# One weight matrix unevenly over the DMA engines, and a new order of the last tiles, in a decode block bound by its loads

## The chip, the cores and the metric

One core of one Trainium2 chip. The time is the device time of one execution in microseconds; a kernel's time is the median of its runs. The span is that of the profiled execution from its first to its last instruction, 1.5 to 2 us less than the time of the same execution.

## The reference

A decode step with one new token for each of 4 sequences: layer norm, then attention against a cache of 8,192 positions with 32 heads of 128, and beside it a gated feed-forward layer; both are added to x.

```python
xn = layernorm(x)                                    # x: 4 x 512
q = (xn @ wq) as (4, 32 heads, 128)                  # wq: 512 x 4096
p = softmax(einsum("bhqd,bhkd->bhqk", q, k_cache) * 128 ** -0.5)
o = einsum("bhqk,bhkd->bhqd", p, v_cache)            # caches: 4 x 32 x 8192 x 128 each
out = x + o @ wo + (silu(xn @ w_gate) * (xn @ w_up)) @ w_down
```

All inputs are bf16. The two caches are 537 MB of the 551 MB that have to be read.

## The kernel before

Everything large goes through five slots of 4 MiB. A tile n is one sequence's K or V for a pair of heads; there are 64 of each. All loads are issued on one queue, in the order of the code. K tiles come two iterations ahead of their scores, V tiles two iterations ahead of their products.

```python
wq_t = slot()                                            # 512 rows: 4 on each partition
nc.sync.dma_start(out=wq_t[:], in_=A_wq.rearrange("(p c) n -> p (c n)", c=EC))
...
for c in range(EC):                                      # q: 32 matmuls 128x32x512
    for half in range(NH):
        for cg in range(NQ):
            mm(q_ps[half][cg * QB:(cg + 1) * QB, :], xnt_w[:, c, :], wq_t[:, n0:n0 + 512], start=(c == 0))
...
for i in range(NT + LP):                                 # NT = 64, LP = 2
    if i + 2 < NT:
        load_k(i + 2)
    nv = i + 2 - LP
    if 0 <= nv < NT:                                     # the last two V tiles come in pieces
        load_v(nv, (32, 32, 32, 16, 16) if nv == NT - 1 else (32,) * 4 if nv == NT - 2 else (T,))
    ...                                                  # per tile: 8 DVE transposes, 32 score matmuls
    npv = i - LP                                         # 32 matmuls p x V of tile i - 2
    ...
        if bv == B - 1 or npv == NT - 2:
            fin_1(jv)                                    # ACT copy, DVE mask and sum: o of a pair of heads
        if bv == B - 1:
            fin_q(jv)                                    # PE sums over rows: waits for fin_1
```

## Time and profile before

| | before |
|---|---|
| time | 1288.93 us (1288.72 to 1289.07, 3 runs) |
| span | 1287.1 us |
| PE, DVE busy | 84%, 57% |
| bytes read | 550.8 MB |
| PE's wait for the DVE sum of o | 37.3 us in 16 places |

The prediction below shows the lines that carry the argument and reads them. The core has 16 DMA engines, and the profile's DMA line is the mean busy share of the 16. The trace also has every packet's start, duration, size and queue, but not its engine. On one engine a packet starts 3 or 4 ns before the recorded end of its predecessor, so the packets can be strung into 16 chains; those of the kernel before hold the same sequence of sizes each, 34.42 MB of kernel data. "Last data of an engine" below is the end of the last input packet of such a chain. This regrouping is worked out from the records; it is not a view of the profile.

### The profile page before, as it was taken

The page shows a single profiled execution, that of the slowest core. Times are in us where ns is not written, and L with a number is a line of the kernel's source. Part 1 is how long each engine was busy: PE and PEld are TensorE (multiplying, and loading weights), DVE is VectorE, ACT ScalarE, POOL GpSimd, SP SyncE. Part 2 cuts the span into 40 slices and gives each one's busy share as a digit, 9 for nine tenths or more (in the row PEclk, how much of TensorE's full clock was granted, in tenths as well). Part 3 has the DMA queues.
Part 4 walks back from the last instruction along what each step waited for, and adds up shares of the span by engine and source line. Part 5 has one row for each costly group of instructions (what it writes and reads, how often), then busy time and mean ns, then how long its engine had stood idle before and what let it go on. Part 6 is the DMA issues. An engine that isn't in the chain of part 4 may idle for free.

```text
span 1287.1 us, 11189 instructions
## 1 busy us (share of the span) xinstructions
PE 1083.1 (84%) x4778; PEld 430.3 (33%) x4778; DVE 738.1 (57%) x951; ACT 39.7 (3%) x87; POOL 5.3 (0%) x13
## 2 busy tenths in 40 slices
PE   4888888888888798897997888888887988978788
PEld 1334333333333333332333333333333333333334
DVE  6663556546556556466556566465465465573544
ACT  1000000000000000000000000000000000000000
POOL 1000000000000000000000000000000000000000
PEclk9898898998989999898998989989899898989899
DMA  9999999999999999999999999999999999999997
GB/s 407 427 430 435 437 425 437 429 436 431 432 435 428 436 432 433 431 432 435 431 435 428 434 432 431 436 431 433 430 434 431 437 430 432 433 431 427 433 434 304
DMA packets 21529, 551.49 MB, mean 428 GB/s; under 512 B 2268, under 2 KB 2792, under 8 KB 3944
## 3 DMA queue, kind: packets, MB, share of 16 engines
q1 hardware_dynamic: 21464, 550.78, 99.4%
q8 instruction: 37, 0.61, 0.2%
q14 instruction: 12, 0.10, 0.0%
q10 hardware_dynamic: 16, 0.01, 0.0%
HBM read 550.77 MB, written 0.00 MB: 428 GB/s over the span
## 4 chain that ended last, share of the span: by engine, by line
DMA 50%; PE 31%; DVE 14%; issue 5%; ACT 1%; SPq 0%; DVEq 0%
DMA slot<-in_A_k_cache_dram 44%; PE oacc L76 17%; PE sps L76 12%; DVE kt L277 11%; DMA slot<-in_A_v_cache_dram 6%; PE mps L76 1%; DVE ptz L318 1%; DVE o L356 1%; PE xps L76 1%; DVE o_sb L354 1%; ACT o_sb L353 0%; PE mps L299 0%; DVE otn L377 0%; PE yo_ps L76 0%; DVE rcp L328 0%
## 5 line engine op out<-in xcount | busy, mean ns | idle before, releaser
L76 PE MATMUL sps<-kt,zq 128*128 128x512 bf16 x2048 | 578.3, 421 | 145.2 <-DVE kt L277 128.7
L277 DVE STREAM_TRANSPOSE kt<-slot 128x1024 uint32<-128x1024 uint32 x512 | 587.6, 1210 | 90.4 <-DMA slot<-in_A_k_cache_dram 89.5
L76 PE MATMUL oacc<-slot,ptz 128*8 128x512 bf16 x2016 | 450.4, 379 | 0.4 <-DMA slot<-in_A_v_cache_dram 0.4
L76 PEld LDWEIGHTS <-zq 128*128 128x128 bf16 x2048 | 212.0, 104 | 496.1 <-issue 317.0
L76 PEld LDWEIGHTS <-ptz 128*8 128x8 bf16 x2016 | 177.5, 92 | 258.1 <-issue 27.8
L328 DVE RECIPROCAL rcp<-mps 128x4 f32<-128x4 f32 x32 | 5.9, 183 | 281.9 <-PE mps L76 281.9
L354 DVE TENSOR_TENSOR o_sb<-o_sb,rowu 128x512 f32<-128x512 f32 x16 | 11.1, 693 | 89.2 <-ACT o_sb L353 89.0
L76 PE MATMUL xps<-rowy,o 128*32 128x4 f32 (+1 forms) x228 | 13.5, 205 | 37.3 <-DVE o L356 37.3
L293 DVE TENSOR_REDUCE mx<-sps 128x1 f32<-128x512 f32 x32 | 22.1, 692 | 18.5 <-PE sps L76 18.5
L76 PEld LDWEIGHTS xps<-rowy,o 128*32 128x32 f32 (+1 forms) x228 | 12.1, 154 | 44.9 <-DVE o L356 44.9
L268 DVE COPY zq<-qt 32x8 bf16<-32x8 bf16 x128 | 21.3, 166 | 1.3
L302 DVE TENSOR_REDUCE nm<-mps 128x4 f32<-128x64 f32 x32 | 7.2, 225 | 24.0 <-PE mps L299 24.0
L356 DVE TENSOR_REDUCE o<-o_sb 128x128 f32<-128x512 f32 x16 | 16.3, 1020 | 0.5
L76 PEld LDWEIGHTS mps<-rowb,rs 128*128 128x128 f32 x64 | 9.5, 186 | 13.8 <-issue 13.8
L76 PEld LDWEIGHTS <-slot 128*128 128x128 bf16 x272 | 11.7, 126 | 3.5 <-DVE slot L188 2.6
L76 PE MATMUL mps<-rowb,rs 128*128 128x4 f32 x64 | 12.3, 263 | 0.0
L353 ACT COPY o_sb<-oacc 128x512 f32<-128x512 f32 x16 | 9.4, 586 | 76.8 <-PE oacc L76 76.8
L377 DVE TENSOR_TENSOR otn<-xps,rcp 32x16 bf16<-32x16 f32 x28 | 4.8, 170 | 11.7 <-PE xps L76 10.3
L299 PE MATMUL mps<-ident_f,mx 128*128 128x128 f32 x32 | 10.3, 323 | 0.8 <-DVE mx L293 0.8
L299 PEld LDWEIGHTS mps<-ident_f,mx 128*128 128x128 f32 x32 | 4.3, 133 | 14.7 <-DVE mx L293 14.2
L170 PE MATMUL xps<-ident,kt 4*128 4x4 bf16 x4 | 0.3, 173 | 10.1 <-DVE kt L165 10.1
L76 PE MATMUL yo_ps<-slot,otn 128*4 128x256 bf16 x64 | 8.2, 281 | 0.3 <-DVE otn L366 0.3
(150 smaller groups left out, 148.5 us busy)
## 6 DMA issues: line engine op xcount, KB each, us to landing
slot<-in_A_k_cache_dram SPq DMA_DIRECT2D x64, 4096.0 KB, 39.2
slot<-in_A_v_cache_dram SPq DMA_DIRECT2D x62, 4096.0 KB, 36.8
slot<-in_A_v_cache_dram SPq DMA_DIRECT2D x7, 1024.0 KB, 22.3
slot<-in_A_wq_dram SPq DMA_DIRECT2D x1, 4096.0 KB, 12.3
slot<-in_A_wo_dram SPq DMA_DIRECT2D x1, 3584.0 KB, 40.2
slot<-in_B_w_gate_dram SPq DMA_DIRECT2D x1, 1792.0 KB, 31.9
slot<-in_B_w_up_dram SPq DMA_DIRECT2D x1, 1792.0 KB, 35.8
slot<-in_B_w_down_dram SPq DMA_DIRECT2D x1, 1792.0 KB, 30.9
```

Source lines behind the costliest of these rows:

```text
L76: nc.tensor.matmul(out_ap, lhsT=lhsT, rhs=rhs, start=start, stop=True, skip_group_check=True, **kw)
L268: nc.vector.tensor_copy(out=zq[gr % 2][a * QB:(a + 1) * QB, :, :, XO + a * QB].rearrange("p b (j r) -> p r j b", r=2), in_=qt[a * QB:(a + ...
L277: nc.vector.transpose(out=kt[:].bitcast(dt.uint32).rearrange("p (j t r) -> p t j r", j=2, r=QB), in_=src.rearrange("p (t j r) -> p t j r", ...
L293: nc.vector.reduce_max(out=mx[:], in_=s_ps[gr][:], axis=AX.X)
L299: nc.tensor.matmul(mps[:, 0:P], lhsT=nmx.pop(gr)[:, 0:1].to_broadcast([P, P]), rhs=ident_f[:, :], is_transpose=True, start=True, stop=True ...
L302: nc.vector.tensor_reduce(out=nm[:], in_=by_row(mps[:, 0:P]), axis=AX.XY, op=ALU.max, negate=True)
L318: nc.vector.transpose(out=t_[y * HP:(y + 1) * HP, :, y, :, :].rearrange("p s u x -> p s (u x)"), in_=p_[y * HP:(y + 1) * HP, :].rearrange( ...
L328: nc.vector.reciprocal(out=rcp[j][:, :, 2 * bp:2 * bp + 2], in_=mps[:, P:P + B].rearrange("p (y b) -> p y b", y=HT))
L353: nc.scalar.copy(out=o_sb[:].rearrange("p u d -> p (u d)"), in_=o_acc[j % 2][:])
L354: nc.vector.tensor_tensor(out=o_sb[:], in0=o_sb[:], in1=rowu[:].unsqueeze(2).to_broadcast([P, NV, Dh]), op=ALU.mult)
L356: nc.vector.reduce_sum(out=o1[:], in_=o_sb[:].rearrange("p u d -> p d u"), axis=AX.X)
L377: nc.vector.tensor_tensor(out=otn[q0:q1, blk * 4:blk * 4 + 4, :], in0=xps[q0:q1], in1=r_[q0:q1, y, :].unsqueeze(1).to_broadcast([QB, 4, B] ...
```

## The change

It has four parts. wq is no longer spread evenly: 384 rows and 32 rows lie on all partitions, and 96 rows lie on 32 partitions alone, loaded by two transfers whose outermost source dimension is 4. The last four tiles to be loaded are V tiles (K63 moves ahead of V60), the last two in other pieces. The PE part of o of a pair of heads is put off until after three pieces of the next scores. wo is loaded four iterations sooner, and the row sums of p are taken one iteration sooner.

```diff
-    wq_t = slot()
-    nc.sync.dma_start(out=wq_t[:], in_=A_wq.rearrange("(p c) n -> p (c n)", c=EC))
+    C1, LE, LG, LR, NC = EC - 1, 4, 2, 3, 4
+    LW = 4 * LE
+    R1, R2 = C1 * P, C1 * P + LG * LW * LR
+    wq_t, wq_u = slot(), slot()
+    nc.sync.dma_start(out=wq_t[:, 0:C1 * NQ_], in_=A_wq[0:R1, :].rearrange("(p c) n -> p (c n)", c=C1))
+    nc.sync.dma_start(out=wq_t[:, C1 * NQ_:C1 * NQ_ + CN], in_=A_wq[R2:D, :].rearrange("r (k n) -> (r k) n", k=NC))
+    for g in range(LG):
+        r0 = R1 + g * LW * LR
+        nc.sync.dma_start(out=wq_u[g * QB:g * QB + LW, 0:LR * NQ_],
+                          in_=A_wq[r0:r0 + LW * LR, :].rearrange("(r e c) n -> e r (c n)", r=4, e=LE))
...                                        (x laid out to match; 80 projection matmuls, q in two sums)
-    R_FFN, R_WO = 5, NT - 5
+    R_FFN, R_WO = 5, NT - 9
-        nv = i + 2 - LP
+        nv = i + 2 - LP if i < NT - 4 else -1 if i == NT - 4 else i + 1 - LP
-            load_v(nv, (32, 32, 32, 16, 16) if nv == NT - 1 else (32,) * 4 if nv == NT - 2 else (T,))
+            load_v(nv, (64, 32, 16, 8, 8) if nv == NT - 1 else (64, 64) if nv == NT - 2 else (T,))
...
+                if g == 2:
+                    while late:
+                        late.pop(0)()
...
-        npv = i - LP
+        npv = i - LP if i < NT - 2 else -1 if i == NT - 2 else i - LP - 1
...
-                    fin_q(jv)
+                    late.append(lambda jv=jv: fin_q(jv))
```

More of the change, by code (lines that the diff above doesn't have):

```diff
@@ L86 @@
     nc.scalar.dma_start(out=x_sb[:], in_=x_flat[:, :])
-    wq_t = slot()
-    nc.sync.dma_start(out=wq_t[:], in_=A_wq.rearrange("(p c) n -> p (c n)", c=EC))
+    NQ_ = H * Dh
+    C1, LE, LG, LR, NC = EC - 1, 4, 2, 3, 4
+    LW = 4 * LE
+    R1, R2 = C1 * P, C1 * P + LG * LW * LR
+    CN = NQ_ // NC
+    assert D - R2 == P // NC
+    wq_t, wq_u = slot(), slot()
[5 more added lines that the diff above has]
+                          in_=A_wq[r0:r0 + LW * LR, :].rearrange("(r e c) n -> e r (c n)", r=4, e=LE))
     k_tiles, v_tiles = {}, {}
@@ L121 @@
         nc.gpsimd.memset(z_[:], 0.0)
-    xnt_w = const.tile([P, EC, QB], dt.bfloat16, name="xnt_w")
+    NF = EC + C1 + NC
+    NX = NF + LR
+    xnt_w = const.tile([P, NX, QB], dt.bfloat16, name="xnt_w")
     nc.gpsimd.memset(xnt_w[:], 0.0)
@@ L163 @@
     nc.vector.reciprocal(out=rstd[:], in_=std[:])
-    xn_bf = kt_pool.tile([B, D], dt.bfloat16, name="kt")
-    nc.vector.tensor_scalar(out=xn_bf[:], in0=xc[:], scalar1=rstd[:, 0:1], scalar2=None, op0=ALU.mult)
-    xnt_ps = psX.tile([P, EC, B], dt.bfloat16, name="xps")
-    for c in range(EC):
-        nc.tensor.transpose(xnt_ps[:, c, :], xn_bf[0:B, c:D:EC], ident[0:B, 0:B])
-    nc.vector.tensor_copy(out=xnt_w[:, :, 0:B], in_=xnt_ps[:])
+    xn_bf = kt_pool.tile([B, D + NC * P + LG * LW * LR], dt.bfloat16, name="kt")
@@ new lines @@
+    nc.vector.memset(xn_bf[:, D:D + NC * P], 0.0)
+    nc.vector.tensor_scalar(out=xn_bf[:, 0:D], in0=xc[:], scalar1=rstd[:, 0:1], scalar2=None, op0=ALU.mult)
+    DQ = D + NC * P
+    for k in range(NC):
+        nc.vector.tensor_copy(out=xn_bf[:, D + k * P + k:D + (k + 1) * P:NC], in_=xn_bf[:, R2:D])
+    for g in range(LG):
+        r0 = R1 + g * LW * LR
+        nc.vector.tensor_copy(
+            out=xn_bf[:, DQ:DQ + LG * LW * LR].rearrange("b (c g e r) -> b g c e r", c=LR, g=LG, e=LE)[:, g],
+            in_=xn_bf[:, r0:r0 + LW * LR].rearrange("b (r e c) -> b c e r", r=4, e=LE))
@@ new lines @@
+    xnt_ps = psX.tile([P, NX, B], dt.bfloat16, name="xps")
+    cols = [slice(c, D, EC) for c in range(EC)] + [slice(c, R1, C1) for c in range(C1)]
+    cols += [slice(D + k * P, D + (k + 1) * P) for k in range(NC)]
+    for c in list(range(EC, NX)) + list(range(EC)):
+        if c < NF:
+            nc.tensor.transpose(xnt_ps[:, c, :], xn_bf[0:B, cols[c]], ident[0:B, 0:B])
+        else:
+            for g in range(LG):
+                c0 = DQ + ((c - NF) * LG + g) * LW
+                nc.tensor.transpose(xnt_ps[g * QB:g * QB + LW, c, :], xn_bf[0:B, c0:c0 + LW], ident[0:B, 0:B])
@@ L174 @@
+    nc.vector.tensor_copy(out=xnt_w[:, 0:NF, 0:B], in_=xnt_ps[:, 0:NF, :])
+    for g in range(LG):
+        nc.vector.tensor_copy(out=xnt_w[g * QB:g * QB + LW, NF:NX, 0:B], in_=xnt_ps[g * QB:g * QB + LW, NF:NX, :])
     NH = H * Dh // 512 // NQ
     q_ps = [psS.tile([P, 512], dt.float32, name="sps") for _ in range(NH)]
-    for c in range(EC):
-        for half in range(NH):
-            for cg in range(NQ):
-                n0 = c * H * Dh + (half * NQ + cg) * 512
-                mm(q_ps[half][cg * QB:(cg + 1) * QB, :], xnt_w[:, c, :], wq_t[:, n0:n0 + 512], start=(c == 0))
@@ L182, with q_mm @@
-    q_bf = slots.tile([P, NH, 2, 8, NQ, QB], dt.bfloat16, name="slot")
+    def q_mm(acc, nb, c, p0, p1, w, start=False):
+        half, cg = divmod(nb, NQ)
+        mm(acc[half][cg * QB:(cg + 1) * QB, :], xnt_w[p0:p1, c, :], w, start=start)
+    for c in range(C1):
+        for nb in range(NH * NQ):
+            q_mm(q_ps, nb, EC + c, 0, P, wq_t[:, c * NQ_ + nb * 512:c * NQ_ + (nb + 1) * 512], start=(c == 0))
+    for nb in range(NH * NQ):
+        k, n0 = divmod(nb * 512, CN)
+        q_mm(q_ps, nb, EC + C1 + k, 0, P, wq_t[:, C1 * NQ_ + n0:C1 * NQ_ + n0 + 512])
@@ new lines @@
+    for g in range(LG):
+        p0, p1 = g * QB, g * QB + LW
+        for c in range(LR):
+            for nb in range(NH * NQ):
+                q_mm((q_ps, o_acc)[g], nb, NF + c, p0, p1, wq_u[p0:p1, c * NQ_ + nb * 512:c * NQ_ + (nb + 1) * 512],
+                     start=(g == 1 and c == 0))
+    q_2 = kt_pool.tile([P, NH, 512], dt.float32, name="kt")
+    for half in range(NH):
+        nc.scalar.copy(out=q_2[:, half, :], in_=o_acc[half][:])
+    q_bf = wq_u[:, 3 * NQ_:4 * NQ_].rearrange("p (n r x c i) -> p n r x c i", n=NH, r=2, x=8, c=NQ)
@@ L183 @@
     for half in range(NH):
         for par in range(2):
-            src = q_ps[half][:].rearrange("p (x i r) -> p x i r", x=8, r=2)[:, :, :, par]
-            src = src.unsqueeze(2).to_broadcast([P, 8, NQ, QB])
-            if half == 0:
-                nc.vector.tensor_copy(out=q_bf[:, half, par], in_=src)
-            else:
-                nc.scalar.copy(out=q_bf[:, half, par], in_=src)
+            a_, b_ = [t_.rearrange("p (x i r) -> p x i r", x=8, r=2)[:, :, :, par].unsqueeze(2).to_broadcast([P, 8, NQ, QB])
+                      for t_ in (q_ps[half][:], q_2[:, half, :])]
@@ L192 @@
+            nc.vector.tensor_tensor(out=q_bf[:, half, par], in0=a_, in1=b_, op=ALU.add)
     qt_ps = psM.tile([P, NH, 2, 8, NQ * B], dt.float32, name="mps")
@@ L385 @@
     JL = H // HT - 2
-    R_FFN, R_WO = 5, NT - 5
+    R_FFN, R_WO = 5, NT - 9
     wo_next, wo_ready = 0, 0
+    late = []
     build_q(0)
-    for i in range(NT + LP):
+    for i in range(NT + LP + 1):
         if i + 2 < NT:
             load_k(i + 2)
-        nv = i + 2 - LP
+        nv = i + 2 - LP if i < NT - 4 else -1 if i == NT - 4 else i + 1 - LP
         if 0 <= nv < NT:
-            load_v(nv, (32, 32, 32, 16, 16) if nv == NT - 1 else (32,) * 4 if nv == NT - 2 else (T,))
+            load_v(nv, (64, 32, 16, 8, 8) if nv == NT - 1 else (64, 64) if nv == NT - 2 else (T,))
         if i == R_FFN - 3:
@@ L428 @@
             jv, bv = divmod(npv, B)
-            if bv % 2 == 0:
-                row_sums(npv // 2)
+            if i < NT and bb == 1:
+                row_sums(gr)
             if bv == B - 1 or npv == NT - 2:
@@ L434, with fin_d @@
                 if jv < JL:
-                    fin_q(jv)
-                    if jv % 2 == 1:
-                        wo_ready = (jv + 1) * HT
-                else:
-                    xps = x_tile()
-                    fin_2(jv, xps)
-                    fin_3(jv, xps)
-                    wo_ready = (jv + 1) * HT
+                    late.append(lambda jv=jv: fin_q(jv))
+                else:
+                    def fin_d(jv=jv):
+                        xps = x_tile()
+                        fin_2(jv, xps)
+                        fin_3(jv, xps)
+                    late.append(fin_d)
+                wo_ready = (jv + 1) * HT if jv >= JL or jv % 2 == 1 else wo_ready
         elif i < NT and bb == 1:
             max_2(gr)
-        if i >= R_WO:
+            row_sums(gr)
+        if i >= R_WO and not late:
             for _ in range(8):
```

## The prediction

> **What bounds the kernel now.** I read the page first, then the DMA share in fine slices of the last 25 us, then the chain that ended last, in order of time, then the trace's single DMA packet records.
>
> ```profile
> span 1287.1 us, 11189 instructions
> PE 1083.1 (84%) x4778; PEld 430.3 (33%) x4778; DVE 738.1 (57%) x951; ACT 39.7 (3%) x87; POOL 5.3 (0%) x13
> ...
> DMA  9999999999999999999999999999999999999997
> ...
> q1 hardware_dynamic: 21464, 550.78, 99.4%
> q8 instruction: 37, 0.61, 0.2%
> q14 instruction: 12, 0.10, 0.0%
> ```
>
> PE is busy 84% of the span, yet DMA is full in every slice but the last. The 550.8 MB of inputs cannot be fewer, so the transfers set the time. What a change can touch is the two ends, and how evenly 16 engines share the bytes. The same DMA line over 1262 to 1287 us alone (0.625 us a slice), and the windows around its step:
>
> ```profile
> DMA  9999999999999999999976555555553200000000
> ```
>
> ```profile
> 1272.00:1274.00 2.00, 2.00 (x12) 0.82 (x9) 0.00 (x0) 0.00 (x0) 0.00 (x0) 1.00 0.99 412
> 1274.00:1276.00 2.00, 2.00 (x11) 0.83 (x10) 0.00 (x0) 0.00 (x0) 0.00 (x0) 1.00 0.75 315
> 1276.00:1278.00 2.00, 2.00 (x10) 0.72 (x8) 0.00 (x0) 0.00 (x0) 0.00 (x0) 1.00 0.56 236
> ```
>
> The columns before the last two are the engines' busy times and the clock; the last two are DMA share and GB/s. The share falls from 1 to 0.56 = 9/16 and stays there for 5 us: seven engines have run out while nine still work. To see why, I regrouped the packet records. On one engine a packet starts 3 to 4 ns before its predecessor's recorded end, so all records fall into 16 chains of 34.42 MB of kernel data each, without idle time between first and last tile. Their last data end as follows (us):
>
> - seven chains with no TensorE instruction fetch: 1274.5 to 1275.7, the typical one 1274.7;
> - eight chains that carry the 37 fetches of 16 KiB in turn (q8): 1280.4 to 1280.6 and 1281.7 to 1282.1, depending on whether 4 or 5 fetches fell before their end;
> - one chain with nine 8 KiB fetches (q14): 1282.37.
>
> (1281.7 - 1274.7) / 5 = 1.4 us per 16 KiB fetch: the fetch is recorded with 0.93 us, and the 32 KiB packet beside it takes 1.7 instead of 1.213 us. **The late nine are late by their instruction fetches, and the slowest engine ends the kernel.** The end of the chain:
>
> ```profile
> 1265.54 17.13 DMA slot<-in_A_v_cache_dram
> 1282.67 0.05 issue
> 1282.71 0.60 PE xps L76 x16
> 1283.32 0.03 issue
> 1283.34 0.18 DVE otn L366
> 1283.52 0.04 issue
> 1283.56 1.03 PE yo_ps L76 x4
> 1284.59 0.02 issue
> 1284.61 0.36 ACT res L458
> ```
>
> From the last data at 1282.37 to the end of the span, 1287.1, there are 4.74 us: 0.34 until PE sees them, 0.60 for 16 small matmuls, 0.2 for normalising, 1.0 for wo, 0.36 for the copy, the rest the output transfer. The execution time, 1288.93, is 1.8 above the span.
>
> [...] No run yet shows which engines; x, with 4 rows, does show 4 data packets. [...] the trace has 32,768 B in 1.210 us (1.213 less the overlap), 27.1 GB/s[...]. [...] after a 10.4 us wait, score matmuls at 1196 us are 0.43 us apart, not 0.22.
>
> **The change, part by part.**
>
> *wq.* Before, 4 MiB lie evenly: 262,144 B per engine. After, 384 rows (24 KiB per partition) and 32 rows (2 KiB per partition) lie evenly, 196,608 + 16,384 = 212,992 B per engine, and 96 rows go in two transfers over four engines, 2 x 4 x 24,576 = 196,608 B more on each of those. So twelve engines have 49,152 B less, at 27.1 GB/s **1.8 us less**; four have 147,456 B more, **5.4 us more**. If the four are early ones, they end at 1274.7 + 5.4 = 1280.1, at worst 1275.7 + 5.4 = 1281.1; the late ones end at 1282.37 - 1.8 = 1280.6 and 1282.1 - 1.8 = 1280.3. I take 1280.7: **1.7 us earlier**. That 5.4 + 1.8 = 7.2 is just the gap of the two groups (7.0 to 7.7) is my main reason to think that the 96 rows were sized for engines known to be early.
>
> *Preparation of q.* 17 small transposes instead of 4, six copies into the padded x and two more copies out, about 1.5 us, beside the wq transfer. 80 instead of 32 projection matmuls at 0.113 us (3.61/32). wq is complete only after 1.8 + 0.8 (slow first packet, 2 us) + 7.3 + 0.6 + 7.3 = 17.8 us instead of 12.7. 24 more matmuls behind it (2.7), two ACT copies (1.2), four adds of about 1.2 us on DVE instead of two copies there and two on ACT: the first K transpose moves from 22.7 to about 30 us. This costs nothing at the end while DMA queues stay filled. Per tile, first packet minus issue was 24 to 31 us for the first eight waiting tiles, 19 at least up to 1150 us, and 7.7 at the very end. A delay of 7 to 9 us that PE makes up by some 3 us per tile pair (19.7 us of DMA against about 16 of PE) leaves 10 us in hand.
>
> *Order of the last tiles.* Before: K62 V60 K63 V61 V62 V63. After: K62 K63 V60 V61 V62 V63, PV one iteration later. Bytes are equal. Before, PE had only 0.48 us of idle time ahead of the last 16 matmuls, so an earlier end of DMA alone would have met a busy PE. After, K63 lands about 39 us before the end (four tiles of 9.8), its scores end near 1250.5; PV60, PV61, PV62 (7.1 each) end near 1258, 1268 and 1275.5, and the first half of V63 comes at 1275.6. PE follows the data. Slots come free about 20 us before they are needed instead of 8 to 13. The last piece is 8 positions, not 16: 8 matmuls of 0.037 us less, **0.3 us**.
>
> *o waits for the next scores.* PE stood 37.3 us in 16 places before the head-sum matmuls, waiting for DVE; that goes to nearly nothing. It is not on the path: DMA is full meanwhile. Likewise row sums and an earlier wo load (four tile pairs sooner, one slot fewer for that time, where 10 us of queue remained before): **0**.
>
> Sum: -1.7 - 0.3 = -2.0 us, so 1288.93 - 2.0 = 1286.9.
>
> **The rivals.**
>
> 1. *The four engines are not the early ones.* If one carries fetches, it ends at 1282.1 + 5.4 = 1287.5, and the kernel takes 1288.93 + 5.1 - 0.3 = about 1294. For it: the records carry no engine numbers. Against: the sizing above; and the first wq packet of an early chain starts 4 ns before the end of an x packet's completion record (1.774 against 1.778), as if on the same engine. 10%.
> 2. *PE becomes the end.* Between PV60 (1258) and V61 (1261) PE idles 3 us. [...] gain cancelled, about 1288.5. [...] 20%.
> 3. *Late start or uneven landing empties the queue.* Engines 0 to 3 now lag by 7.2 us at first; a slot is free only when the slowest engine has landed and the tile is used. If both eat the 20 us in hand, every lost us adds at the end. Against: at least 10 us left. 5%.
> 4. *The 4-engine transfers are hidden anyway*: if the early engines are fewer than thought or a further fetch falls on the last engine[...], 1288 to 1289.
>
> **Range and chances.** Centre 1286.9; a near-exact balance gives 1286, rival 2 or 4 up to 1289, and the wrong engines 1294. Two per cent is 25.8 us, which no rival reaches; only a starved queue through the whole kernel could. Range 1285.6 to 1289.3; faster by over 2% 0.005, within 0.985, slower 0.01.
>
> **What would show it.** In the changed profile, the last slices of DMA should hold near full until about 1278 to 1279 and then fall in one step; three engines idle from 1273, so 13/16 = 0.81 for some 6 us. In chains: twelve with 1.8 us less, four with 5.4 us more and late by 7.2 us in the first tiles. wq's longest landing should come near 17.8 us, the first K transpose near 30 us, PE's wait for the DVE head sum should shrink from 37.3 us to a few, and the last matmuls should be 8 right after a landing. Wrong if DMA shows 12 engines done and 4 working at the end, if gaps appear in the middle of the DMA line, or if the last matmuls run without a wait for DMA.

## The result, and the profile after

| | before | after |
|---|---|---|
| time | 1289.0 us (1288.72 to 1289.39, 4 runs) | 1294.74 us (1294.67 to 1295.06, 4 runs) |
| span | 1287.1 us | 1292.8 us |
| last data of all | 1282.37 us | 1288.20 us |
| from there to the end of the span | 4.74 us | 4.6 us |

(The first table has the three runs of before that were known when the prediction was made.) The ratio is 1.0045, interval 1.0027 to 1.0062. Such ratios are the mean time of one kernel's fast runs over that of the other's of the same rounds, so not quite the ratio of the medians. That counts as the same within 2%, but it is a slowdown clear of noise, where the prediction had a gain of 2.0 us. The whole difference is already there when the last data land: they come 5.83 us later, and the span is 5.7 us longer.

The page of the changed kernel, the lines that answer to those of before:

```profile
span 1292.8 us, 11337 instructions
PE 1089.4 (84%) x4776; PEld 436.5 (34%) x4839; DVE 743.3 (57%) x962; ACT 38.8 (3%) x87; POOL 5.5 (0%) x13
...
DMA  9999999999999999999999999999999999999996
...
q8 instruction: 38, 0.62, 0.2%
q14 instruction: 13, 0.11, 0.0%
```

DMA is still full, and one fetch more has come on each of the two instruction queues. The same DMA line over 1262 to 1287 us, as for before, and then the windows at the end (columns: window, its length, busy time of PE, PEld, DVE, ACT and POOL with instruction counts, clock, DMA share, GB/s):

```profile
DMA  9999999999999999999998999996630100000000
```

```profile
1276.00:1278.00 2.00, 2.00 (x14) 0.89 (x14) 0.00 (x0) 0.00 (x0) 0.00 (x0) 1.00 0.99 413
1280.00:1282.00 2.00, 2.00 (x11) 0.84 (x10) 0.00 (x0) 0.00 (x0) 0.00 (x0) 1.00 0.19 75
1284.00:1286.00 2.00, 2.00 (x62) 1.57 (x61) 0.79 (x2) 0.58 (x1) 0.00 (x0) 1.00 0.06 27
1286.00:1288.00 2.00, 1.30 (x43) 1.20 (x40) 0.92 (x1) 0.00 (x0) 0.00 (x0) 1.00 0.06 25
```

The step of 9/16 is gone: fifteen engines end by 1281. Then 0.06 = 1/16 remains for 7 us, at 25 to 27 GB/s, the rate of one engine (27.1 GB/s in the records of before). **A single engine carries the end.**

In the chains that engine is plain. Four chains hold 34.57 MB, the ones that got the 96 rows. Three of them end at 1279.8, 1280.2 and 1280.7 us. The fourth carries ten fetches of 8 KiB besides, and ends at 1288.20. The other twelve hold 34.37 MB and end between 1278.7 and 1280.8.

That the fifteen end so close together is only in part the balance that was wanted. Four of the twelve have few or no fetches and 1.8 us less to load than before; they should have been done near 1273. In the chains four such engines stand idle once for about 5 us, until about 1104 us, and so end near 1279. The share of DMA shows it too (1098 to 1104 us, before and then after):

```profile
1098.00:1104.00 6.00, 5.94 (x27) 2.23 (x26) 2.28 (x9) 0.78 (x2) 0.00 (x0) 1.00 1.01 437
```

```profile
1098.00:1104.00 6.00, 6.00 (x29) 2.50 (x27) 5.38 (x9) 0.00 (x0) 0.00 (x0) 1.00 0.82 324
```

It happens while wo is loaded in small packets, of 1 and 4 KiB. The issue of the K tile behind it takes 14 us in both kernels (13.99 and 14.30), and in the changed one these engines run out of packets meanwhile. The wq part alone has the same hole, near 1180 us. It doesn't set the end: the late engine and the three others with wq rows have no idle time there.

The end of the chain of waits of the changed kernel (start, length, what):

```profile
1265.21 5.93 PE oacc L76 x27
1271.14 0.31 PE mps L76 x2
1271.45 13.08 PE oacc L76 x64
1284.53 0.02 issue
...
1286.98 2.08 PE xps L76 x66
```

This chain has no wait for DMA at its end, where that of before had 17 us of it. PE ran the products of V61 and V62 until 1284.5 and its last 64 small matmuls until 1289.06, while the last data were there at 1288.20. So two explanations were open: the one late engine, or a tail in which PE itself is late.

The part that puts o off did what it was meant to. PE's matmuls that sum o, before and then after (busy, mean ns, idle time ahead of them in us):

```profile
L76 PE MATMUL xps<-rowy,o 128*32 128x4 f32 (+1 forms) x228 | 13.5, 205 | 37.3 <-DVE o L356 37.3
```

```profile
L76 PE MATMUL xps<-rowy,o 128*32 128x4 f32 (+1 forms) x228 | 13.6, 205 | 0.7 <-DVE o L405 0.7
```

37 us of waiting have gone, and the kernel is not faster: DMA was full meanwhile.

### The profile page after: what moved, and what is told of

The parts are those of the page before. It is cut to its first block, busy times and chain, and to the rows that moved or that the text cites. A ratio compares the mean times of both kernels' runs of the same rounds, so it can differ in the third digit from the quotient of the medians.

```text
span 1292.8 us, 11337 instructions
## 1 busy us (share of the span) xinstructions
PE 1089.4 (84%) x4776; PEld 436.5 (34%) x4839; DVE 743.3 (57%) x962; ACT 38.8 (3%) x87; POOL 5.5 (0%) x13
## 4 chain that ended last, share of the span: by engine, by line
DMA 51%; PE 31%; DVE 13%; issue 5%; ACT 1%; SPq 0%; DVEq 0%
DMA slot<-in_A_k_cache_dram 40%; PE oacc L76 16%; PE sps L76 12%; DMA slot<-in_A_v_cache_dram 11%; DVE kt L326 9%; DVE ptz L367 1%; PE mps L76 1%; DVE o L405 1%; PE xps L76 1%; DVE o_sb L403 1%; ACT o_sb L402 1%; PE mps L348 0%; PE yo_ps L76 0%; DVE otn L426 0%; SPq L102 0%
## 5 line engine op out<-in xcount | busy, mean ns | idle before, releaser
L76 PEld LDWEIGHTS <-zq 128*128 128x128 bf16 x2048 | 217.0, 107 | 521.7 <-issue 346.8
L239 DVE TENSOR_TENSOR slot<-sps,kt 128x1024 bf16<-128x1024 f32 x4 | 4.6, 1216 | 8.7 <-ACT kt L232 8.7
```

Of the source, the lines that this page charges most:

```text
L76: nc.tensor.matmul(out_ap, lhsT=lhsT, rhs=rhs, start=start, stop=True, skip_group_check=True, **kw)
```

## The experiments

Three theories. **Theory 1**: one of the four low-numbered engines also carries the 8 KiB instruction fetches, was already the slowest, and was given 5.4 us more. **Theory 2**: the new tail makes PE late. **Theory 3**: the later start of q, or the uneven landing, empties the queue. Ten kernels ran in three groups; each group shared its runs of the kernel before, whose median lay between 1288.89 and 1288.96. All results were correct.

### The wq part alone

The changed kernel down to the making of q, the kernel before from there on.

```diff
-    R_FFN, R_WO = 5, NT - 9          # and order of tiles, pieces, late o: all as before
+    R_FFN, R_WO = 5, NT - 5
```

> The wq part of the change alone (384 + 32 rows evenly, 96 rows on engines 0 to 3), with the tail, the order of the last tiles and the late o of the kernel before. Theory 1 (one of the four low-numbered engines is the one that also carries the 8 KiB instruction fetches of q14; it gets 5.4 us more and sets the end): its last data near 1288, about 5.5 to 6 us slower than before, so 1294.5 to 1295. Theory 2 (PE bound in the new tail: V62's chunks, the o copy and 64 small matmuls run after the data): this part alone is no slower than before, 1287 to 1289.5. Theory 3 (later start of q empties the queue): slower by the idle DMA time that shows before 200 us.

Measured: 1294.91 us (4 runs), ratio 1.0045 (1.0028 to 1.0062), the whole loss. The engine with 34.57 MB and nine 8 KiB fetches had its last data at 1287.77, 5.40 us later than before; the 147,456 B that it got more are worth 5.44 us at 27.1 GB/s. Here the last matmuls do wait for DMA (end of the chain of waits):

```profile
1270.90 17.19 DMA slot<-in_A_v_cache_dram
1288.09 0.04 issue
1288.13 0.60 PE xps L76 x16
```

Theory 2 is not needed for the loss. Theories 1 and 3 are still open.

### Everything but the wq part

```diff
+    wq_t = slot()                    # wq and q as before
+    nc.sync.dma_start(out=wq_t[:], in_=A_wq.rearrange("(p c) n -> p (c n)", c=EC))
```

> Everything but the wq part: order of the last tiles, pieces 64/32/16/8/8, o after the next scores, earlier wo, with wq as before. Theory 1: within 0.5 us of before, at best 0.3 us faster (1288.4 to 1289.2), and the last matmuls wait for DMA. Theory 2: 1293 or more, with no wait for DMA before the last matmuls.

Measured: 1289.73 us (4 runs) against 1288.96, ratio 1.0004 (0.9989 to 1.0019). The medians differ by 0.8 us, the ratio is not clear of noise. The tail isn't what cost 5.7 us, but it brought none of the 0.3 us expected. In the trace the last data came at 1282.95, 0.58 later, with ten 8 KiB fetches on the latest engine instead of nine; and the span ended 5.05 us after them, not 4.74. Its chain of waits:

```profile
1232.61 0.59 ACT o_sb L353
...
1233.23 0.70 DVE o_sb L354
...
1233.95 1.02 DVE o L356
1234.97 1.15 DVE kt L277
...
1266.21 13.08 PE oacc L76 x64
...
1281.74 2.31 PE xps L76 x66
```

DVE begins the transposes of K62 only at 1234.97, behind the sum of o that it has to do first. The scores of K62 and K63 now follow each other without V products between them and end near 1258.5. V61 and V62 run until 1279.3 without a wait, and the last 64 matmuls run until 1284.05, when the data have been there for a microsecond. PE, which had half a microsecond in hand before, is now last by about as much.

### The same rows over all 16 engines

```diff
-                          in_=A_wq[r0:r0 + LW * LR, :].rearrange("(r e c) n -> e r (c n)", r=4, e=LE))
+                          in_=A_wq[r0:r0 + LW * LR, :].rearrange("(p c) n -> p (c n)", c=LR))
...
-            in_=xn_bf[:, r0:r0 + LW * LR].rearrange("b (r e c) -> b c e r", r=4, e=LE))
+            in_=xn_bf[:, r0:r0 + LW * LR].rearrange("b (e r c) -> b c e r", r=4, e=LE))
```

> The changed kernel, but the 96 rows go to the same 32 partitions over all 16 engines (outermost source dimension 16 instead of 4), so each engine again carries 262,144 B of wq; all compute as in the changed kernel. Theory 1: all of the loss goes, 1288 to 1289.3, and one step of 9/16 comes back in the DMA share at the end. Theory 2 or 3: stays near 1294.7, since PE order and the later q are unchanged.

Measured: 1295.33 us, ratio 1.0048 (1.0033 to 1.0063). Taken at its word this refutes theory 1. But the experiment had brought a cost of its own. Windows of this run, and then of the changed kernel, in which the same bytes go over four engines (last two columns DMA share and GB/s):

```profile
13.00:14.00 1.00, 1.00 (x16) 0.37 (x12) 0.00 (x0) 0.00 (x0) 0.00 (x0) 1.00 1.13 123
14.00:15.00 1.00, 1.00 (x16) 0.26 (x8) 0.00 (x0) 0.00 (x0) 0.00 (x0) 1.00 0.65 74
```

```profile
13.00:14.00 1.00, 1.00 (x15) 0.32 (x11) 0.00 (x0) 0.00 (x0) 0.00 (x0) 1.00 0.97 418
14.00:15.00 1.00, 1.00 (x16) 0.30 (x8) 0.00 (x0) 0.00 (x0) 0.00 (x0) 1.00 1.12 483
```

DMA engines count as busy, but only 74 to 123 GB/s move. In the packet records the 24 KiB packets of the second of the two transfers take 3.4 to 3.6 us each and those of the first 1.5 to 3.4, against the 0.912 us that they take in the changed kernel. On sixteen engines, 16 packets of 24,576 B in 3.6 us are 109 GB/s; on four, in the changed kernel, 4 in 0.912 us are 108 GB/s. So sixteen moved no more than four. Why was not shown: no run here tells one reason from another. In any case all engines were held up, not four: the seven without many fetches ended at 1280.4 to 1281.2 instead of 1274.5 to 1275.7, the rest 5 to 6 us later than before too. The run says nothing for or against theory 1. It shows that these 32 partitions gain nothing from sixteen engines instead of four.

### Which engine is which

```diff
+        if 6 <= i < 22:                          # in the kernel before
+            k = i - 5
+            nc.sync.dma_start(out=pad_t[0:k, 4 * k - 4:4 * k], in_=A_wq[0:k, 0:4])
```

> A label run, not for time: the kernel before with 16 tiny transfers of k rows of 8 B, k = 1 to 16, one in each of 16 iterations. If a transfer with k rows runs on the lowest k engines, the 16 chains of packets carry 16, 15, ... 1 of these tiny packets, which numbers them. Theory 1: of engines 0 to 3 exactly one is the chain with the 8 KiB fetches, the other three carry no 16 KiB fetches. If all four are free of fetches, theory 1 falls.

Measured: one look, 1289.4 us (state unknown, as for any single run). The 16 chains hold 16, 15, ... 1 of the tiny packets, each count once, so each chain has a place in one fixed order. The engine numbers here are that order: engine 0 is the chain with 16 of them, engine 15 the one with 1. So the transfer of four rows ran on engines 0 to 3. Their last data:

| engine | instruction fetches before its last data | last data, us |
|---|---|---|
| 0, 2, 7, 8, 15 | none | 1274.6 to 1274.9 |
| 1 | one of 8 KiB | 1275.4 |
| 4 | two of 8 KiB | 1275.8 |
| **3** | **nine of 8 KiB** | **1282.3** |
| 5, 6, 9 to 14 | 4 or 5 of 16 KiB each | 1280.4 to 1282.1 |

Engines 0, 1 and 2 are free or nearly so. Engine 3 is not. The four lowest engines are three early ones and a late one.

### Three engines instead of four

The wq part alone with one line altered; tail and sum of bytes stay. Compute doesn't quite: with 4 rows on each of the 24 partitions, 96 projection matmuls take the place of 80.

```diff
-    C1, LE, LG, LR, NC = EC - 1, 4, 2, 3, 4
+    C1, LE, LG, LR, NC = EC - 1, 3, 2, 4, 4
```

> As the wq part alone, but the 96 rows go over three engines instead of four (outermost source dimension 3, 12 partitions a group, 4 rows each): by the label run engines 0 to 2, all without the many 8 KiB fetches, which sit on engine 3. Compute and byte totals stay. Engines 0 to 2 get 262,144 B extra, net 212,992 / 27.1 = 7.9 us more than before, ending at 1274.8 + 7.9 = 1282.6 to 1283.3; engine 3 and the rest 1.8 us less. Theory 1 (engine 3 alone made the loss): 1289 to 1290, some 5 us faster than the wq part alone. Theory 3 (the later q or the uneven load as such): 1294 or more, since the three lag by even more at first.

Measured: 1289.68 us (4 runs), ratio 1.0005 (0.999 to 1.0021): 5.2 us less than with four engines, though the three now lag by about 10 us in the first tiles and q comes even later (first K transpose at 31.31 us, against 28.15 in the wq part alone). The three ended at 1282.5 to 1283.0 (34.64 MB each), engine 3 with its nine fetches at 1280.2. Theory 3 falls, theory 1 holds. DMA over 1262 to 1287 us:

```profile
DMA  9999999999999999999997777776411111000000
```

### The same one line in the changed kernel

> The changed kernel with one line altered: the 96 rows on engines 0 to 2 (4 rows on each of 24 partitions) instead of 0 to 3. New tail, late o and late q stay. Theory 1 (engine 3 with its fetches made the loss): engines 0 to 2 end near 1282.6 to 1283.0, engine 3 near 1281; 1289.3 to 1290.2, some 5 us faster than the changed kernel. Theory 2 (the new tail on PE): stays at 1293 or more.

Measured: 1289.81 us (4 runs), ratio 1.0005 (0.9989 to 1.0022), 4.9 us less than the changed kernel, with the new tail, the late o and the late q all in place. Engines 0 to 2 ended at 1282.3 to 1282.8, engine 3 with ten fetches at 1281.2.

### Fetches added on purpose

To the kernel before, in each of 64 iterations, ten tiny DVE instructions; and as a control one that takes DVE about as long.

```diff
+            for _ in range(10):                  # 640 in all
+                nc.vector.memset(pad_t[:, 0:2], 0.0)
```

```diff
+            nc.vector.memset(big_t[:], 0.0)      # the control: 64 in all, 128x512 fp32
```

> The kernel before with 640 tiny DVE instructions more, ten in each of 64 iterations (640 x 64 B = 40 KiB, 5 fetches of 8 KiB). Theory 1 says that the fetches sit on the engine that ends last: 14 to 15 instead of 9 or 10 fetches, 5 x 0.85 = 4.2 us later, about 1293.2. If instruction fetches don't set the end, the time stays at 1289, DVE being idle 43% of the time.

> Control for the 640 instructions: 64 DVE memsets of 512 fp32 each, one in each iteration, about 0.5 us of DVE time per iteration like the ten tiny ones, but 4 KiB of instructions only (at most one fetch more). Theory 1: 1289 to 1289.9. If it is DVE's time and not the fetches that costs, it is as slow as the 640.

Measured: 1295.36 us with the 640, ratio 1.0051 (1.0037 to 1.0064); 1289.62 us with the 64, ratio 1.0005 (0.9991 to 1.0019). The 8 KiB queue of the first and of the second:

```profile
q14 instruction: 17, 0.14, 0.0%
```

```profile
q14 instruction: 13, 0.11, 0.0%
```

Before it was 12, so five more and one more: 640 instructions brought 40 KiB, 64 B each, as the expectation had it. In the chains all of these fell on the engine that ended last: 14 and 10 instead of 9. Its last data came at 1286.63, that is 4.26 us later than before, or 0.85 us a fetch, as expected; with the control at 1283.19, 0.82 later. DVE's own time is not what costs: it is busy for 766.7 us in the control and for 772.1 with the 640. The 640 cost 2.1 us more than I had worked out: the span ended 6.8 us after the last data instead of 4.74, again with V products and small matmuls on PE and no wait for DMA at the end of its chain. So PE was late too; whether by the later tiles or by the ten instructions ahead of the transposes is not separated. At 64 B the 37 fetches of 16 KiB in the kernel before are 9,472 instructions. Only TensorE has so many there (4,778 matmuls and as many weight loads), so these are called TensorE's: an estimate, as no run altered them.

### A balanced version

48 rows on three engines (2 rows on each of 24 partitions), the other 80 as 64 + 16 over all partitions; first with the tail of before, then with the new one.

```diff
-    C1, LE, LG, LR, NC = EC - 1, 4, 2, 3, 4
+    C1, LE, LG, LR = EC - 1, 3, 2, 2
+    FAM = (2, 8)                                 # 64 rows in halves, 16 rows in eighths
+    NC = sum(FAM)
...                                               (loads, layout of x and matmuls for both parts)
```

> A balanced version: 48 rows on three engines (2 rows on 24 partitions), 64 + 16 of the remaining rows evenly, tail as before. Engines 0 to 2 end at 1274.8 + 3.9 = 1278.7 to 1279.4, all others 0.9 us sooner, engine 3 at about 1281.5. Theory 1: 0.9 us faster than before, 1288.0 to 1288.4. Theory 3: no gain or a loss from the later q.

> The balanced 48 rows on engines 0 to 2 with the changed kernel's tail. Against the same wq part with the tail of before (1288.4): theory 1 alone says the same or 0.3 us less (8 matmuls fewer behind the last data), if PE is ready; from the tail-alone run, where PE ran its last 64 matmuls after the data had landed, I expect instead 0.3 to 1 us more, 1288.6 to 1289.4, and no wait for DMA before the last matmuls.

Measured: 1288.37 us (5 runs), ratio 0.9995 (0.9983 to 1.0008), with the tail of before; 1288.71 us (4 runs), ratio 0.9998 (0.9983 to 1.0013), with the new tail. The first one's last data came at 1281.48, 0.9 us sooner, on engine 3 as expected. Its runs (1288.19 to 1288.48) all lie below the runs of before of the same group (1288.66 to 1289.35), but the interval of the ratio holds 1: it clearly beats the changed kernel, while its 0.6 us against the kernel before are not clear of noise. With the new tail the last data came at 1282.25, with a tenth 8 KiB fetch, and PE again had no wait for DMA at the end.

## Why the prediction was wrong, point by point

**What bounds the kernel: right.** The engine that ends last ends the kernel. That instruction fetches made nine of sixteen late was read from the records of before; the 640 added instructions showed it as a cause for the one with the 8 KiB fetches, at the 0.85 us each that these records give. For the eight with 16 KiB fetches it stays a reading: no run altered their number on purpose.

**The size of the wq part: right.** The prediction said 5.4 us more for four engines and 1.8 less for twelve. Three of the four ended at 1279.8 to 1280.7, where it had 1280.1 to 1281.1. The eight with 16 KiB fetches came out at 1280.8 at the latest, where it had 1280.3 for them.

**Which engines they are: this step failed.** It reads: "If the four are early ones, they end at 1274.7 + 5.4 = 1280.1, at worst 1275.7 + 5.4 = 1281.1". Three are early; engine 3 is the one that carries nine 8 KiB fetches, the very chain that the prediction lists with 1282.37, the latest of all. It got the 5.4 us on top: 1282.37 + 5.44 = 1287.8, measured 1287.77 with nine fetches and 1288.20 with ten. The reason that the prediction gave, that 5.4 + 1.8 just fills the gap of the two groups, is true and still no evidence of where the bytes land: an exact size says that somebody balanced, not that he knew all four. The other reason, an x packet whose end fits the start of an early chain, spoke of one engine of four.

**The first rival was what happened.** It was put at about 1294 with a chance of 10%; measured 1294.74. Its condition, "if one carries fetches", was the right one, and a run that numbers the engines was all that was missing.

**What the DMA line should have shown: wrong.** The prediction had 13/16 = 0.81 for some 6 us from 1273, with three engines idle; with engine 3 among the four it would have been four, and 0.75. Measured was 0.99 at 1276 to 1278, because these four had already stood idle near 1100 us. The third rival, an emptied queue, so came true in part. It took nothing from the end, as the engine that ended last was never idle. Two of the prediction's own signs of being wrong did appear: a gap in the middle, and last matmuls without a wait for DMA.

**The tail: wrong in a small way.** The 0.3 us for a shorter last piece didn't come. The prediction had the scores of K63 end near 1250.5 and the products of V62 near 1275.5; with wq as before they ended near 1258.5 and at 1279.3. It left out that DVE first does the sum of o of the pair before, and that two tiles of scores then follow each other. So PE was not through when the last data came, and what followed them took 5.05 us instead of 4.74. The tail alone took 0.8 us more than before, the balanced version 0.3 us more with it than without; neither is clear of noise, and both had one fetch more on engine 3. Where the data come late enough the shorter piece may pay: in the changed kernel 4.6 us follow the last data, in its wq part alone 4.8.

**The further fetch** that the prediction mentions as a way to lose came on both queues. On engine 3 an added 8 KiB fetch costs 0.85 us where it falls before the last data, measured with five at once. Where one came unasked, the last data were 0.4 to 0.8 us later (the changed kernel against its wq part, the tail alone, the control of 64 memsets, the balanced version).

**The late q and the late o: right.** The first K transpose began at 27.95 us (predicted about 30, before 22.69). Tiles still waited 13 us and more in the queue in the first 200 us, so nothing was lost there. PE's 37.3 us of waiting went to 0.7 and bought nothing.

What stays open: which 8 KiB fetch falls when. The changed kernel had ten before its last data and its wq part alone nine, with 962 DVE instructions in both. Open too is why the four early engines ran dry near 1100 us; with the rows on three engines they idled 0.7 us at most.

## What to carry to other kernels

When DMA is full from end to end, ask which of its engines ends last and what else it carries, before moving bytes between them; here the sixteen transfers of 1 to 16 rows told that in one run. Instruction fetches were such a load: one of 16 KiB made its engine about 1.4 us later by the records, one of 8 KiB 0.85 us, and nine of sixteen engines ended 5.7 to 7.7 us after the typical early one. Bytes may be shifted only onto engines that are known to be early, each of them, because one late engine among four can lose all that twelve others gain: here, with the wq part alone, 1.8 us less on twelve and the last data 5.40 us later. And time taken from an engine off the path, such as 37 us of PE waits here, is worth nothing by itself.
